# Passes shared with GpSimd and a planner that lets VectorE and GpSimd overlap, in a fused attention and two-layer kernel

## The chip, the cores and the metric

The kernel runs on one core of one Trainium2 chip. The metric is device time in microseconds (us) of one execution, and a variant is judged by the median of its runs. TensorE (PE in the profile, PEld for its weight loads) multiplies matrices, VectorE (DVE) and ScalarE (ACT) work element by element, GpSimd (POOL) does the same on tiles in SBUF, and SyncE (SP) issues all the DMAs.

## The reference

Attention over 4 batches and 8 heads, 576 positions of 64 values, with a causal window of 128 and a bias that falls linearly with distance; then a layer with a softmax gate and a normalisation over 1024 hidden values; then a gated layer with 2048 hidden values.

```python
def _attn_ref(q, k, v):
    scores = scale * np.matmul(q, k.transpose(0, 1, 3, 2))
    bias = slopes[:, None, None] * (-np.abs(rel).astype(np.float32))[None, :, :]
    mask = (rel >= 0) & (rel < window)
    scores = np.where(mask, scores + bias[None], -1000000000.0)
    attn = np.exp(scores - np.max(scores, axis=-1, keepdims=True))
    attn = attn / (np.sum(attn, axis=-1, keepdims=True) + 1e-09)
    return np.matmul(attn, v)

def _moe_ref(x, w_in, w_out, g_ln):          # 2304 tokens, 512 -> 1024 -> 512
    h = x @ w_in
    e = np.exp(h - np.max(h, axis=-1, keepdims=True))
    solu = h * (e / (np.sum(e, axis=-1, keepdims=True) + 1e-09))
    mu = np.mean(solu, axis=-1, keepdims=True)
    var = np.mean((solu - mu) ** 2, axis=-1, keepdims=True)
    return (((solu - mu) / np.sqrt(var + 1e-06)) * g_ln) @ w_out

def _moe2_ref(x, w_in, w_out):               # 2304 tokens, 512 -> 2048 -> 512
    h = x @ w_in
    return (h * (1.0 / (1.0 + np.exp(-h)))) @ w_out
```

## The kernel before

**Tiles.** The 2304 tokens are 18 blocks of 128 rows. A block goes through scores (`a_qk`), a pass that adds the bias and finds the row maximum (`a_max`), the exponential, a transposition of the weights (`a_parts`), the product with the values (`a_av`), a division (`a_evac`), the first matrix product (`m1_in`) and the normalisation (`layer_norm`). Two blocks form a chunk for `m1_out`, `m2_in` and `m2_out`.

**Splitting.** Each float32 operand of a large product is held as two half-precision tiles: the high part is a copy to half precision, the low part is what the copy left over. Three half-precision products then stand for one float32 product. So almost every tile passes through a "copy" (the helper `copy`, or `scaled` where a scale is applied) and a "low part" (the helper `combine`, a subtraction of two SBUF tiles, or a `scalar_tensor_tensor` of VectorE that scales and subtracts at once).

**Weights.** The weights come as 8-byte floats. `load_weight` loads 48 tiles into `stage` buffers, `decode` turns each into float32 (ScalarE L456, VectorE L458 and L460; one pair goes wholly through VectorE, L464 to L468), TensorE and VectorE compute a bound for the scale, and `split_weight` splits the tile: E_W says whether slot b takes the two-pass form of VectorE (`wh`, then L533) or the three-pass form (`wc` scales in place, `wh` copies, `wl` subtracts). Slots 0 to 7 are `w0`, 8 to 15 `w8`, 16 to 31 `w16`, 32 to 47 `w32`.

**Who does what, and in which order.** All work is entered into a list with its reads and writes. A planner in the program (`Sched.solve`) gives every piece to an engine and a place in that engine's order, by priorities (RANK, SLOPE, LATER by kind of work and block) and by a cost for each piece. PICK fixes the engine of most pieces: one letter per tile, V for VectorE, A for ScalarE, G for GpSimd. On the chip each engine works through its own order; semaphores make it wait for data. The planner before keeps one time, `port`, for pieces marked as holding a port that VectorE and GpSimd share: a marked piece of either engine begins only when the marked piece before it has ended:

```python
t = max(free[o.eng], o.ready, port if held else 0)
...
if held:
    port = t + o.cost
```

Marked are all of GpSimd's large passes, VectorE's copies and scalings, its subtractions in `combine`, and the `scalar_tensor_tensor` low parts. The decoding pass L460 is not marked, though it too reads two SBUF tiles.

**Lines that the steps below touch.** L342, L343: copies on ScalarE and VectorE. L347, L348, L350: scaled copies on ScalarE, VectorE, GpSimd. L354, L355: subtractions on VectorE and GpSimd. L533, L642: scale-and-subtract of weights and of values on VectorE. L688, L773: score and value products. L714: bias and maximum. L820, L920, L957, L984: the four large products.

Of the kernel before, what the change touches and what calls it, by code (L numbers as in the profile page):

```python
# [69 lines left out]

class Sched:
# [108 lines left out]
    def solve(self):  # L182
        free = {e: 580 for e in ("PE", "V", "A", "G", "SP")}
        dma_free = port = 0
# [31 lines left out]
        while n_left:  # L216
# [82 lines left out]
def fused_kernel(ctx, tc, qk, qn, kn, vt, rel, w_in, w_out, g_ln, w2_in, w2_out, out):  # L299
# [3 lines left out]
    s = Sched()  # L303
# [12 lines left out]
    def cv(n, fast=False):  # L316
        return 68 + (0.52 if fast else 1.045) * n
# [10 lines left out]
    def v(n, fn, r=(), w=(), fast=False, port=False):  # L328
        s.op([("V", cv(n, fast), fn, port or fast)], r, w)
# [30 lines left out]
    def transpose(fn, r=(), w=(), blocks=8):  # L360
        s.op([("SP", 1294, fn, False)], r, w, dma=165 * blocks)
# [81 lines left out]
    def decode(st, slot, j):  # L443
# [4 lines left out]
        def high():  # L448
            return st[:, :, 1]
# [4 lines left out]
        if DECODE[j // 2] == "A":  # L454

            act(512, lambda: A.activation(high().bitcast(F32), high().bitcast(F32), AF.Prelu,  # L456
# [3 lines left out]
            v(530, lambda: V.scalar_tensor_tensor(out=out(), in0=high(), scalar=3, in1=low(),  # L460
# [59 lines left out]
    def split_weight(name, slot0, n, cols, per_k=None):  # L520
        for j in range(n):
            def go(j=j):
# [8 lines left out]
                if E_W[b] == "V":  # L531
# [3 lines left out]
                      [(W, a), (W, b), src], [(W, b)], port=True)  # L535
# [100 lines left out]
    def v_split(i):  # L636
# [187 lines left out]
    def layer_norm(i):  # L824
# [120 lines left out]
    def m2_in(c, j):  # L945
# [18 lines left out]
        def flat(x):  # L964
# [83 lines left out]
    for c in range(NB // 2 + 1):  # L1048
# [7 lines left out]
        while n < until:  # L1056
# [12 lines left out]
RANK = {"aturn": 8190.5, "av": 1566.9, "evac": -3109.3, "exp": 5884.2, "gate": -1711.8, "in": -283.0, "in2": 763.1,  # L1069
        "load": -4397.6, "lparts": -1653.6, "max": 176.2, "max1": 339.6, "norm": -7961.4, "out": -1027.6,  # L1070
        "out2": 3298.4, "parts": -1379.1, "qk": 1402.7, "s0": -168.5, "s16": 369.8, "s32": 455.6, "s8": 3931.6,
        "share": -1605.8, "store": 2439.7, "table": -5196.2, "tav": 59.2, "tevac": -749.8, "texp": 4157.2,
        "tpar": 3201.3, "tscore": -1216.6, "tsub": 333.9, "vload": 753.3, "vnorm": -2520.6, "vsplit": 128.2,
        "w0": 1479.2, "w16": 76.9, "w32": 998.7, "w8": -63.2, "xturn": -869.5, "y": -1911.0}
SLOPE = {"aturn": 47.79, "av": -25.89, "evac": -5.68, "exp": 11.77, "gate": -21.88, "in": 36.34, "in2": -11.62,
         "load": 10.3, "lparts": 18.87, "max": -24.94, "max1": -2.34, "norm": -4.0, "out": 15.06, "out2": 30.48,
         "parts": -23.26, "qk": 32.18, "s0": 3.76, "s16": 1.95, "s32": 6.94, "s8": 26.54, "share": 17.85,
         "store": -34.37, "table": 17.51, "tav": -5.62, "tevac": 7.06, "texp": 19.15, "tpar": 25.04, "tscore": 5.66,
         "tsub": 13.31, "vload": 7.87, "vnorm": 15.99, "vsplit": 25.91, "w0": -6.05, "w16": 1.69, "w32": -8.51,
         "w8": -8.24, "xturn": 39.68, "y": -12.6}  # L1080
LATER = {("aturn", 1): 9.1, ("aturn", 2): -2.6, ("aturn", 3): 1.2, ("aturn", 6): -7.3, ("aturn", 7): -20.1,
         ("aturn", 9): -30.2, ("aturn", 11): -27.9, ("aturn", 12): -248.5, ("aturn", 13): 191.9, ("aturn", 14): 79.9,
         ("aturn", 15): -4.4, ("aturn", 16): 72.7, ("aturn", 17): -73.0, ("av", 0): -2.3, ("av", 1): -8.5,
         ("av", 2): 62.3, ("av", 5): 6.7, ("av", 6): 108.7, ("av", 8): -92.5, ("av", 12): 253.9, ("av", 13): -61.2,
         ("av", 16): -7.0, ("av", 17): 102.8, ("evac", 2): 2.1, ("evac", 3): 92.2, ("evac", 4): -25.0,
         ("evac", 5): -116.6, ("evac", 6): 0.4, ("evac", 7): -7.5, ("evac", 9): 269.9, ("evac", 12): 6.4,
         ("evac", 15): 61.8, ("evac", 16): 20.0, ("exp", 0): -2.6, ("exp", 1): -9.0, ("exp", 2): -239.6,
         ("exp", 4): 1.4, ("exp", 6): 95.0, ("exp", 8): 86.1, ("exp", 9): 34.4, ("exp", 10): 55.1, ("exp", 11): 11.9,
         ("exp", 12): -10.3, ("exp", 13): -121.4, ("exp", 14): 75.2, ("exp", 15): -38.3, ("exp", 16): 40.2,
         ("exp", 17): 91.8, ("gate", 2): -17.8, ("gate", 4): -56.2, ("gate", 10): -39.9, ("gate", 12): 66.8,  # L1090
# [138 lines left out]
```

## Time and profile before

| what | value |
|---|---|
| median of 3 runs | 731.22 us (730.71 to 733.2) |
| profiled execution, its own time | 729.44 us |
| its span in the profile | 727.5 us |
| TensorE's mean granted clock in it | 0.981 |
| instructions | 13956 |

The profile shows one execution. Its busy times are of each engine alone and overlap with each other; the table of stretches shows in which part of the run an engine is nearly always busy. A duration on VectorE or GpSimd includes time in which the instruction has begun and cannot go on, so the same instruction with the same shape is compared at its median and at its mean.

### The profile page before, as it was taken

The page shows a single profiled execution, that of the slowest core. Times are in us where ns is not written, and L with a number is a line of the kernel's source. Part 1 is how long each engine was busy: PE and PEld are TensorE (multiplying, and loading weights), DVE is VectorE, ACT ScalarE, POOL GpSimd, SP SyncE. Part 2 cuts the span into 40 slices and gives each one's busy share as a digit, 9 for nine tenths or more (in the row PEclk, how much of TensorE's full clock was granted, in tenths as well). Part 3 has the DMA queues.
Part 4 walks back from the last instruction along what each step waited for, and adds up shares of the span by engine and source line. Part 5 has one row for each costly group of instructions (what it writes and reads, how often), then busy time and mean ns, then how long its engine had stood idle before and what let it go on. Part 6 is the DMA issues. An engine that isn't in the chain of part 4 may idle for free.

```text
span 727.5 us, 13956 instructions
## 1 busy us (share of the span) xinstructions
PE 674.3 (93%) x5541; PEld 464.0 (64%) x5541; DVE 444.8 (61%) x1125; ACT 346.2 (48%) x738; POOL 138.5 (19%) x140
## 2 busy tenths in 40 slices
PE   4563688999999999999999999999999999999997
PEld 2432367778565577667766676678566777657853
DVE  3899999996897747553556657547672523321220
ACT  5687668575646635444454445525341422231231
POOL 1223034322443312130322112101010200100000
PEclk9996799999999999999999999999999999999999
DMA  9999985593535534251723454334250421100000
GB/s 309 346 247 273 241 199 134 131 231 89 99 78 103 130 73 81 53 114 31 145 59 73 82 107 90 91 56 73 44 102 1 68 65 30 30 30 1 1 30 29
DMA packets 142209, 75.82 MB, mean 104 GB/s; under 512 B 126656, under 2 KB 126784, under 8 KB 142144
## 3 DMA queue, kind: packets, MB, share of 16 engines
q1 hardware_dynamic: 142144, 74.94, 44.2%
q8 instruction: 43, 0.70, 0.4%
q14 instruction: 22, 0.18, 0.1%
HBM read 39.52 MB, written 4.72 MB: 61 GB/s over the span
## 4 chain that ended last, share of the span: by engine, by line
PE 79%; DVE 14%; ACT 3%; issue 2%; DMA 1%; POOL 0%; DVEq 0%; POOLq 0%; ACTq 0%
PE mm L984 25%; PE mm L957 23%; PE mm L920 12%; PE mm L820 11%; PE sa L688 4%; DVE W L460 3%; PE mm L773 2%; DVE stage L458 2%; DVE e L714 1%; PE gram L396 1%; DVE W L533 1%; PE sa L773 1%; DVE W L354 1%; DMA aT<-a 1%; DVE W L348 1%
## 5 line engine op out<-in xcount | busy, mean ns | idle before, releaser
L957 PE MATMUL mm<-y,W 128*128 128x256 f16 x1728 | 210.4, 273 | 1.1 <-DVE t L967 0.7
L984 PE MATMUL mm<-W,g 128*128 128x512 f16 x864 | 204.9, 379 | 0.0
L957 PEld LDWEIGHTS <-W 128*128 128x128 f16 x1728 | 167.0, 98 | 39.8 <-issue 2.0
L984 PEld LDWEIGHTS <-g 128*128 128x128 f16 x864 | 81.8, 98 | 78.7 <-issue 0.2
L820 PE MATMUL mm<-W,xT 128*128 128x512 f16 x432 | 105.2, 390 | 1.7 <-DVE xT L569 1.0
L920 PE MATMUL mm<-lnT,W 128*128 128x256 f16 x864 | 104.8, 273 | 0.0
L920 PEld LDWEIGHTS <-W 128*128 128x128 f16 x864 | 84.0, 98 | 19.7 <-issue 0.5
L719 ACT ACTIVATE e<-e,mx 128x256 f32<-128x256 f32 (+1 forms) x144 | 70.0, 487 | 45.9 <-DVE mx L714 43.3
L970 DVE SCALAR_TENSOR_TENSOR g<-t,g 128x512 f16<-128x512 f32 x72 | 55.5, 774 | 53.7 <-ACT g L969 53.3
L355 POOL TENSOR_TENSOR a<-e,a 128x512 f16<-128x512 f32 (+1 forms) x45 | 54.9, 1222 | 143.2 <-ACT a L342 65.8
L969 ACT ACTIVATE g<-t 128x512 f16<-128x512 f32 x72 | 45.0, 626 | 72.6 <-PE mm L984 61.1
L967 DVE SCALAR_TENSOR_TENSOR t<-t,mm 128x512 f32<-128x512 f32 x72 | 48.7, 682 | 48.3 <-ACT t L966 48.3
L966 ACT ACTIVATE t<-mm,cs 128x512 f32<-128x512 f32 x72 | 48.1, 680 | 62.5 <-PE mm L957 58.6
L820 PEld LDWEIGHTS <-xT 128*128 128x128 f16 x432 | 42.7, 100 | 47.6 <-issue 4.6
L688 PE MATMUL sa<-k,q 64*128 64x128 f32 x544 | 49.4, 312 | 17.1 <-DVE mx L714 12.2
L714 DVE CUSTOM_DVE_ANT_0 e<-sa,table 128x256 f32<-128x256 f32 (+1 forms) x144 | 53.9, 400 | 11.3 <-PE sa L688 6.3
L688 PEld LDWEIGHTS sa<-k,q 64*128 64x128 f32 x544 | 38.5, 202 | 29.1 <-DVE mx L714 15.7
L928 DVE SCALAR_TENSOR_TENSOR y<-mm,cs,y 128x512 f16<-128x512 f32 x18 | 13.3, 748 | 57.1 <-ACT y L925 57.1
L834 DVE TENSOR_REDUCE lnst<-mm 128x1 f32<-128x1024 f32 x18 | 22.0, 1220 | 42.0 <-PE mm L820 42.0
L848 POOL TENSOR_SCALAR lnst<-lnst 128x1 f32<-128x1 f32 x17 | 3.5, 203 | 214.0 <-ACT mm L845 214.0
L925 ACT ACTIVATE y<-mm,cs 128x512 f16<-128x512 f32 x18 | 12.2, 686 | 64.0 <-PE mm L920 56.3
L773 PEld LDWEIGHTS <-aT 128*128 128x128 f16 x816 | 32.9, 101 | 15.2 <-issue 8.6
(151 smaller groups left out, 707.9 us busy)
## 6 DMA issues: line engine op xcount, KB each, us to landing
stage<-in_moe_w_in_dram SPq DMA_DIRECT2D x24, 512.0 KB, 5.3
stage<-in_moe_w_out_dram SPq DMA_DIRECT2D x24, 512.0 KB, 4.5
k<-in_kn_dram SPq DMA_DIRECT2D x18, 256.0 KB, 2.9
q<-in_qn_dram SPq DMA_DIRECT2D x18, 256.0 KB, 3.1
vraw<-in_vt_dram SPq DMA_DIRECT2D x18, 256.0 KB, 3.8
out_dram<-t SPq DMA_DIRECT2D x18, 256.0 KB, 2.3
aT<-a SPq DMA_TRANSPOSE x72, 3.3
lnT<-ln SPq DMA_TRANSPOSE x34, 3.2
```

Of the source, the lines that this page charges most:

```text
L355: ("G", cg(n), lambda: G.tensor_tensor(dst(), a(), b(), op), True)], r, w, pick=pick)
L688: T.matmul(SA[:, j, off + sl * P:off + (sl + 1) * P], q[rows, p, :], k[rows, p, :], start=True, stop=sl not in blank)
L714: v(n + 20, lambda j=j: V.tensor_tensor_reduce(e[:, j, lo:lo + n], SA[:, j, off + lo:off + lo + n], table[:, 2 * p + j, o:o + n], -0.125, ...
L719: act(n, lambda j=j: A.activation(e[:, j, lo:lo + n], e[:, j, lo:lo + n], AF.Exp, bias=mx[:, j:j + 1], scale=-1.0, accum_out=rs[:, 2 * p + ...
L773: T.matmul(heads(i)[:, h // 4, h % 4, :], t[:, (2 * ha + j) * nh + c, :], vb[sl][:, h, hv, :], start=(n == 0), stop=(n == 3 * nh - 1))
L820: T.matmul(pt[:, half * 512:(half + 1) * 512], x[:, hx, k, :], W16(2 * k + half, hw), start=(k == 0 and hx + hw == 0), stop=(k == KD - 1 a ...
L920: T.matmul(pt[:, ct % 2], W16(8 + k, hw)[:, ct * P:(ct + 1) * P], l[:, hx * KF1 + k, :], start=(k == 0 and hw + hx == 0), stop=(k == KF1 - ...
L957: T.matmul(pt[:, mm], W16(16 + 4 * k + m // 4, hw)[:, (m % 4) * P:(m % 4 + 1) * P], y[:, hx, k, :], start=(k == 0 and hw + hx == 0), stop= ...
L966: act(512, lambda: A.activation(t.tile, flat(pt.tile), AF.Tanh, scale=cs[:, 0:1]), [pt, (cs, 0)], [t], extra=1)
L967: v(512, lambda: V.scalar_tensor_tensor(out=t.tile, in0=t.tile, scalar=1.0, in1=flat(pt.tile), op0=ALU.add, op1=ALU.mult), [t, pt], [t])
L970: v(512, lambda: V.scalar_tensor_tensor(out=flat(g[:, 1]), in0=t.tile, scalar=2.0 ** -16, in1=flat(g[:, 0]), op0=ALU.mult, op1=ALU.subtrac ...
L984: T.matmul(pt.tile, g[:, hg, mm, b * P:(b + 1) * P], W16(32 + m, hw), start=(m == 0 and hg + hw == 0), stop=(m == KF2 - 1 and hg == 1))
```

## The change

Copies of five kinds (`wh`, `ah`, `xh`, `lh`, `vg`) may go to GpSimd, as a `tensor_scalar` that multiplies by one twice. For blocks 0 to 5 (V_SPLIT is G) `v_split` has three passes instead of two: scale in place (`vc`), copy (`vg`), subtract (`vl`), each on the engine that PICK names. `m2_in` gets the same form for the gate, which GATE = "VVVVVVVVV" leaves unused. The planner drops `port`: VectorE and GpSimd begin when they are free, and a VectorE piece that begins while a GpSimd pass runs is charged a share of its own cost (1.0 for copies and scalings, 0.6 for subtractions, nothing for `scalar_tensor_tensor`), at most for as long as GpSimd's pass still lasts. Some costs in the planner change a little. PICK, E_W, ROOT, NORM, V_AT, RANK, SLOPE and LATER get new values, so the order of the work on every engine is a new one. No product of TensorE is added or removed, and the loads from HBM and transpositions are the same in number.

```diff
+SHARED_FAST, SHARED = 1.0, 0.6
@@ solve
-        dma_free = port = 0
+        dma_free = pool_until = 0
-                begins = max(free[other[0]], o.ready, port if other[3] else 0)
-                if begins + other[1] < max(t, port if alt[3] else 0) + alt[1]:
+                if max(free[other[0]], o.ready) + other[1] < t + alt[1]:
                     alt = other
-            o.eng, o.cost, o.fn, held = alt
-            t = max(free[o.eng], o.ready, port if held else 0)
+            o.eng, o.cost, o.fn, shares = alt
+            t = max(free[o.eng], o.ready)
+            if o.eng == "V":
+                o.cost += shares * min(o.cost, max(0.0, pool_until - t))
             o.done, o.start = True, t
             free[o.eng] = t + o.cost
-            if held:
-                port = t + o.cost
+            if o.eng == "G" and shares:
+                pool_until = t + o.cost
@@ copy
-              ("V", cv(n, True), lambda: V.tensor_copy(dst(), src()), True)], r, w, pick=pick)
+              ("V", cv(n, True), lambda: V.tensor_copy(dst(), src()), SHARED_FAST)] +
+             ([("G", cg1(n), lambda: G.tensor_scalar(dst(), src(), 1.0, 1.0, ALU.mult, ALU.mult), True)]
+              if pick[0] in ("wh", "ah", "xh", "lh", "vg") else []), r, w, pick=pick)
@@ v_split
+        if V_SPLIT[i] == "G":
+            scaled(("vc", i), 512, lambda: r.tile, lambda: r.tile, lambda: sv.tile, [r, sv], [r], True)
+            copy(("vg", i), 512, lambda: t[:, :, 0, :], lambda: r.tile, [r], [(t, 0)])
+            combine(("vl", i), 512, ALU.subtract, lambda: t[:, :, 1, :], lambda: r.tile, lambda: t[:, :, 0, :],
+                    [r, (t, 0)], [(t, 1)])
+            return
...
-E_W = "GGGGGGVGGVVGVVGGVGGVVGGVGVGGGGGVGVVGGGGVGVVGGGGG"
+E_W = "GVGGGGVGGVVGVVGGVGGGVGGVGVGGGGGVGVVGGGVVVVVGGGGG"
-ROOT = "GGGGGGGGGGGGGGVGGG"
-NORM = "VAAAGAAAGGAVVAVGGV"
+ROOT = "GGGGGGGVVGGGGGVGGG"
+NORM = "VAAAGAVAGGAGGVVVGV"
-PICK = {"wc": "AVGAAAAAAAAVAAGAAGAGAVAAAAAAAVGAVGAGGAVAGVAAAAGV",
-        "wh": "VAAAAAAAVAAAAVVVAAAVAVAVAAVAAVAAVVAAVAVAAVVVVAAA",
-        "wl": "VVVGVVGVGGGVGGGGGGGVGVGGGGGVGGVGGGGGVGVGVVGGGVVV", "vh": "AVAAAAVVAVAAVAVVVA",
-        "ah": "VAVAAVAVAAAAVVAVAAAVVAAAAAAVAVAVVVAAVVAVVVVVAAVVVVVVAVAVVAVAAVVAAVVVVVVV",
-        "al": "VGVGGGGGGGGVGGVGVGGVGGGVGGGGGGVGGVGGGVVGGGGVGVGVGGGGGVVVGVVGGVGVVGVVVGVV", "xh": "VAAAAVAVAAAAVVVVAA",
-        "xl": "GGGGGVVGVGGVVVVVVG", "lh": "VAVAVVVVVAAVVAVVVA", "ll": "V.VGVGGGGGGGGVGVGG"}
+PICK = {"vc": "VVAAAAAAAAAAAAAAAA", "vg": "AGAAAGAAAAAAAAAAAA", "vl": "GVGGGGGGGGGGGGGGGG",
+        "gl": "GGGGGGGGGGGGGGGGGGGGGGGGGGGGGGGGGGGGGGGGGGGGGGGGGGGGGGGGGGGGGGGGGGGGGGGG",
+        "wc": "VVAAGGAGAAAVAAAGAAAAAGAAVAGVVGAAAGAGVGVAVVAAVGGG",
+        "wh": "VVAGAAAAAAAVAAVVAAAVAAAAVAVGAVGAVAAGGGAVVVAGVAVA",
+        "wl": "VVGVGGGGGGGVGGVGGGGVGVGGGGGGVGVGVGGGVGVGVVGGGGGV", "vh": "AVAAAAAAAVAAVAVVAA",
+        "ah": "GGVVAGAAAGGAGVGGVGAVAVVGGGAAVGVAVVAAVVAVVVVVAAVVVVVVAVAAVAVAAVVAAVVVVGVV",
+        "al": "GVGGGGVGGGVVGGGGGVGGGGVGGVVVGVGGGVGGGVVGVGGVGVGVGGGGVVVVGVVGGVGVVVVVVGVV", "xh": "VAAAAGAAAAAAVVVVAA",
+        "xl": "GGGGVVGGVGGVGVVVVG", "lh": "VAVGAGGGVAAVVAVVVA", "ll": "V.GGVGGGGGGGGVGVGG"}
+V_SPLIT = "GGGGGGVVVVVVVVVVVV"
+GATE = "VVVVVVVVV"
-V_AT = [0, 1, 9, 10]
+V_AT = [0, 1, 5, 8]
```

## Rows read from the trace of the kernel before

**Rows 1.** The profile's page: busy us, share of the span, instructions.

```profile
PE 674.3 (93%) x5541; PEld 464.0 (64%) x5541; DVE 444.8 (61%) x1125; ACT 346.2 (48%) x738; POOL 138.5 (19%) x140
```

**Rows 2.** Busy time by stretch: from:to, length, busy us of each engine.

```profile
core 0: us, PE busy (x) PEld busy (x) DVE busy (x) ACT busy (x) POOL busy (x), PEclk, DMA share, GB/s
0.00:20.00 20.00, 7.87 (x53) 5.72 (x53) 8.30 (x38) 12.37 (x33) 2.42 (x15) 1.00 0.97 313
20.00:100.00 80.00, 48.96 (x394) 30.84 (x394) 75.55 (x200) 56.21 (x120) 19.75 (x19) 0.85 0.97 270
100.00:168.00 68.00, 62.48 (x602) 48.80 (x601) 66.79 (x158) 47.37 (x99) 23.40 (x21) 0.97 0.64 156
168.00:700.00 532.00, 531.28 (x4381) 366.90 (x4380) 289.41 (x723) 223.92 (x479) 92.97 (x85) 1.00 0.34 68
700.00:727.50 27.50, 23.70 (x122) 11.73 (x120) 4.74 (x7) 6.31 (x10) 0.00 (x0) 1.00 0.10 39
```

**Rows 3.** Groups of PE in 0 to 168 us: idle time before, releasers.

```profile
L688 PE MATMUL sa<-k,q 64*128 64x128 f32 x168 | 20.3, 364 | 17.1 <-DVE mx L714 12.2 <-DMA q<-in_qn_dram 5.0
...
L396 PE MATMUL gram<-W 128*128 128x128 bf16 x148 | 15.6, 252 | 10.9 <-DVE W L460 6.3 <-DVE sv L439 1.5 <-DVE accw2in L401 1.5
L773 PE MATMUL sa<-vs,aT 128*128 128x64 f16 x192 | 10.3, 214 | 7.0 <-DVE mx L714 6.7 <-DMA aT<-a 0.2
```

**Rows 4.** Timeline from 34 to 39 us: start, duration, instruction.

```profile
34.26 1.15 POOL L355 TENSOR_TENSOR a<-e,a 128x512 f16<-128x512 f32 x1
...
34.49 1.19 DVE L343 CAST a<-e 128x512 f16<-128x512 f32 x1
...
35.61 0.41 DVE L343 CAST x<-xm 128x512 f16<-128x512 f32 x1
```

**Rows 5.** Groups in 0 to 168 us by form: busy us, mean ns.

```profile
L460 DVE SCALAR_TENSOR_TENSOR W<-stage 128x512 uint32<-128x512 uint32 x46 | 35.9, 790 | 0.9 <-ACT stage L456 0.4
...
L458 DVE TENSOR_SCALAR stage<-stage 128x512 uint32<-128x512 uint32 x46 | 22.2, 488 | 0.0
...
L354 DVE TENSOR_TENSOR W<-W 128x512 f16<-128x512 f32 x10 | 8.2, 816 | 0.0
...
L533 DVE SCALAR_TENSOR_TENSOR W<-W,sw2in 128x512 f16<-128x512 f32 x6 | 5.8, 986 | 0.4 <-ACT W L347 0.4
...
L343 DVE CAST a<-e 128x512 f16<-128x512 f32 x7 | 3.7, 524 | 0.0
...
L466 DVE SCALAR_TENSOR_TENSOR W<-stage,W 128x512 uint32<-128x512 uint32 x2 | 3.1, 1528 | 0.0
```

**Rows 6.** Tile stage: durations ns min/median/max, first and last start.

```profile
L458 DVE TENSOR_SCALAR stage<-stage x46: 367/417/1380, 15.4 to 166.2; 128x512 uint32<-128x512 uint32 x46
L460 DVE SCALAR_TENSOR_TENSOR W<-stage x46: 670/680/2049, 16.0 to 167.1; 128x512 uint32<-128x512 uint32 x46
...
L468 DVE SCALAR_TENSOR_TENSOR W<-stage,W x2: 672/674/676, 159.4 to 166.5; 128x512 uint32<-128x512 uint32 x2
```

**Rows 7.** Single lines, 0 to 168 us: durations ns min/median/max.

```profile
L343 DVE CAST W<-W x7: 405/410/415, 39.7 to 136.9; 128x512 f16<-128x512 f32 x7
...
L354 DVE TENSOR_TENSOR W<-W x10: 673/676/1565, 40.4 to 136.3; 128x512 f16<-128x512 f32 x10
...
L533 DVE SCALAR_TENSOR_TENSOR W<-W,sw2in x6: 734/747/1640, 115.6 to 140.3; 128x512 f16<-128x512 f32 x6
...
L348 DVE TENSOR_SCALAR W<-W,gs x2: 471/474/476, 64.8 to 91.3; 128x512 f32<-128x512 f32 x1, 128x512 f16<-128x512 f32 x1
...
L350 POOL TENSOR_SCALAR W<-W,gs x1: 686/686/686, 59.9 to 59.9; 128x512 f32<-128x512 f32 x1
...
L355 POOL TENSOR_TENSOR W<-W x11: 1153/1161/2058, 46.6 to 137.4; 128x512 f16<-128x512 f32 x11
...
L642 DVE SCALAR_TENSOR_TENSOR vs<-vraw,sv,vs x5: 737/739/744, 17.6 to 119.3; 128x512 f16<-128x512 f32 x5
```

**Rows 8.** Groups of the whole run by line: a one-column VectorE pass of the root.

```profile
L859 DVE TENSOR_SCALAR lnst<-lnst 128x1 f32<-128x1 f32 x3 | 0.8, 271 | 0.1
```

**Rows 9.** Granted clock and busy time in one stretch of 20 us.

```profile
60.00:80.00 20.00, 8.92 (x48) 5.27 (x49) 18.80 (x46) 17.21 (x39) 6.21 (x7) 0.50 0.93 231
```

More of the change, by code (lines that the diff above doesn't have):

```diff
@@ L326, in cg1, with v @@
         return 215 + 1.05 * n
-    def v(n, fn, r=(), w=(), fast=False, port=False):
-        s.op([("V", cv(n, fast), fn, port or fast)], r, w)
+    def v(n, fn, r=(), w=(), fast=False):
+        s.op([("V", cv(n, fast), fn, SHARED_FAST if fast else 0.0)], r, w)
     def act(n, fn, r=(), w=(), extra=0):
@@ L360, in transpose @@
     def transpose(fn, r=(), w=(), blocks=8):
-        s.op([("SP", 1294, fn, False)], r, w, dma=165 * blocks)
+        s.op([("SP", 1340, fn, False)], r, w, dma=165 * blocks)
     W = Buf(const, [P, NSLOT + LAG, 512], F32, "W")
@@ L454, in decode @@
         if DECODE[j // 2] == "A":
[L456 removed]
+            act(580, lambda: A.activation(high().bitcast(F32), high().bitcast(F32), AF.Prelu,
                                           scale=2.0 ** 16, alpha=-2.0 ** 32), [(st, 0)], [(st, "high")])
@@ L534, in go @@
                                                           op0=ALU.mult, op1=ALU.subtract),
-                      [(W, a), (W, b), src], [(W, b)], port=True)
+                      [(W, a), (W, b), src], [(W, b)])
                     return
@@ L640, in v_split @@
         r = vraw[i]
+        if V_SPLIT[i] == "G":
[4 more added lines that the diff above has]
+            return
         scaled(("vh", i), 512, lambda: t[:, :, 0, :], lambda: r.tile, lambda: sv.tile, [r, sv], [(t, 0)])
         v(640, lambda: V.scalar_tensor_tensor(out=t[:, :, 1, :], in0=r.tile, scalar=sv.tile, in1=t[:, :, 0, :],
-                                              op0=ALU.mult, op1=ALU.subtract), [r, sv, (t, 0)], [(t, 1)], port=True)
+                                              op0=ALU.mult, op1=ALU.subtract), [r, sv, (t, 0)], [(t, 1)])
     kr, qr, es, aT, rsum = {}, {}, {}, {}, {}
@@ L968, in m2_in @@
                                               op1=ALU.mult), [t, pt], [t])
+        if GATE[c] == "G":
+            s.op([("G", cg1(512), lambda: G.tensor_scalar(t.tile, t.tile, 2.0 ** -16, 1.0, ALU.mult, ALU.mult), True)], [t], [t])
+            act(512, lambda: A.activation(flat(g[:, 0]), t.tile, AF.Copy), [t], [(g, 0)])
+            combine(("gl", 8 * c + j), 512, ALU.subtract, lambda: flat(g[:, 1]), lambda: t.tile, lambda: flat(g[:, 0]),
+                    [t, (g, 0)], [(g, 1)])
+            return
         act(512, lambda: A.activation(flat(g[:, 0]), t.tile, AF.Copy, scale=2.0 ** -16), [t], [(g, 0)])
         v(512, lambda: V.scalar_tensor_tensor(out=flat(g[:, 1]), in0=t.tile, scalar=2.0 ** -16, in1=flat(g[:, 0]),
-                                              op0=ALU.mult, op1=ALU.subtract), [t, (g, 0)], [(g, 1)], port=True)
+                                              op0=ALU.mult, op1=ALU.subtract), [t, (g, 0)], [(g, 1)])
     def m2_out(c, j):
@@ L1068 @@
 PITCH = 3.3
[L1069 to L1080, printed above, removed]
@@ new lines @@
+RANK = {"aturn": 8006.1, "av": 1879.0, "evac": -3847.7, "exp": 5373.2, "gate": -3029.2, "in": -1224.6, "in2": 374.3,
+        "load": -1508.8, "lparts": -2952.2, "max": 100.1, "max1": 508.5, "norm": -9709.7, "out": -1383.1,
+        "out2": 3304.4, "parts": -3030.2, "qk": 3092.8, "s0": -578.2, "s16": 532.0, "s32": 708.3, "s8": 2340.0,
+        "share": -2721.5, "store": 801.2, "table": -3894.2, "tav": -525.9, "tevac": -829.2, "texp": 3783.9,
+        "tpar": 3482.1, "tscore": -1673.9, "tsub": 148.6, "vload": 261.1, "vnorm": -2532.6, "vsplit": 1472.5,
+        "w0": 2055.6, "w16": 51.2, "w32": 1203.1, "w8": -344.2, "xturn": -1197.7, "y": -3339.4}
@@ new lines @@
+SLOPE = {"aturn": 49.72, "av": -29.68, "evac": -12.95, "exp": -0.09, "gate": -22.42, "in": 18.84, "in2": -12.17,
+         "load": 26.5, "lparts": 27.05, "max": -24.3, "max1": -24.39, "norm": 37.81, "out": 7.03, "out2": 36.78,
+         "parts": -17.17, "qk": 33.45, "s0": 10.09, "s16": -23.13, "s32": 3.75, "s8": -1.16, "share": -4.92,
+         "store": -14.75, "table": 15.94, "tav": 19.94, "tevac": 3.02, "texp": 13.72, "tpar": 17.57, "tscore": 15.48,
+         "tsub": 27.19, "vload": -0.9, "vnorm": 19.02, "vsplit": 18.14, "w0": -1.68, "w16": 16.51, "w32": -0.54,
+         "w8": -6.38, "xturn": 25.74, "y": -11.26}
```

90 lines of the change are left out of this document (46 added, 44 removed), and 40 rows, old and new, of the table LATER.

## The prediction

> **What bounds the kernel now.** I read the page of the profile first: TensorE is busy 93% of the span, VectorE 61%, GpSimd 19% [rows 1]. These shares hide two stages, so the busy times by stretch come next [rows 2]. From 168 us on TensorE is busy 531.28 of 532 us and VectorE 289.41: TensorE is the bound, and nothing that another engine saves there shows. Before 168 us it is the other way round: TensorE is busy 7.87 + 48.96 + 62.48 = 119.3 of 168 us, which leaves 48.7 us idle, while VectorE is busy 75.55 of 80 and 66.79 of 68 us. The first 20 us are different again: VectorE is busy for 8.30 us, and the DMA share is 0.97. So the run is a head of 168 us in which VectorE holds TensorE back (decoding and splitting the weights, beside the first five blocks), and a tail of some 560 us that is TensorE's. The change removes no product, so the time can fall only by what TensorE's 48.7 idle us in the head shrink (some 4 us at the very end apart), and rise by what they grow. Third, the idle time of TensorE in the head by what ended it [rows 3]: scores wait for the maximum pass of VectorE (12.2 us), value products too (6.7), the sums of squares for the decoding (6.3), together 25.2 us; 5.0 us wait for a load.
>
> Last the timeline, for how VectorE and GpSimd meet [rows 4]. A copy to half precision begins on VectorE at 34.49, while a subtraction of GpSimd runs from 34.26 to 35.41. It takes 1.19 us and ends at 35.68; the next copy of that shape takes 0.41. It is as if it had stood still until GpSimd was done. The durations by form show the same in sum [rows 5 to 7]: a mean above the undisturbed one, times the count, is time lost. L460: 46 x (790 - 680) = 5.1 us; L458: 46 x (488 - 417) = 3.3; L466, against the undisturbed L468: 2 x (1528 - 674) = 1.7; L533: 6 x (986 - 734) = 1.5; L354: 10 x (816 - 676) = 1.4; L343: 7 x (524 - 410) = 0.8. Together 13.8 us of VectorE's 150.6 busy us in the head, beside 2.42 + 19.75 + 23.40 = 45.6 us of GpSimd: 0.30 us of VectorE for each us of GpSimd.
>
> **The change, part by part, in the head.** Undisturbed prices on VectorE [rows 6, 7]: copy 0.41, scaled copy 0.47, subtraction 0.68, scale-and-subtract 0.74; on GpSimd one-input pass 0.69, subtraction 1.16. Half-size tiles count half, tiles of 1024 twice.
>
> Values, blocks 0 to 4 (block 5 comes behind the head): VectorE loses five scale-and-subtracts and one scaled copy (3.70 + 0.47) and gets two scaled copies and one subtraction (0.95 + 0.68): -2.5 us. GpSimd gets one copy and four subtractions: +5.3 us. The split has three passes instead of two: behind a ScalarE pass either way, 0.69 + 1.16 follow in place of 0.74, about a microsecond more before `a_av` may begin. I price this at nothing, since `a_av` also waits for the transposed weights; if that cover is gone it is 1 us for each of five blocks.
>
> Weights, by counting letters of E_W and PICK. `w0`: VectorE 5.7 to 4.2 us, -1.5; GpSimd two scalings, one copy, three subtractions more, +5.5. `w8`: VectorE +0.2, GpSimd -1.2. `w16`: VectorE -0.1, GpSimd three one-input passes, +2.1. `w32` is split behind the head (VectorE is idle nearly half of that time), where I price it at nothing; if it were early, it is some forty passes that trade engines with little net.
>
> Attention weights, blocks 0 to 4: of the copies four go from VectorE to GpSimd, five from ScalarE to GpSimd, two from ScalarE to VectorE, one back: VectorE -1.2, GpSimd +5.5 (nine, two of half size). Of the subtractions five go to GpSimd and four come back: VectorE -0.3, GpSimd +0.6. Normalised tiles: `ll` of block 2 to GpSimd: VectorE -1.4, GpSimd +2.3; `lh` of block 3 from ScalarE to GpSimd: +1.4.
>
> VectorE: -2.5 - 1.5 + 0.2 - 0.1 - 1.2 - 0.3 - 1.4 = **-6.8 us**. GpSimd: 5.3 + 5.5 - 1.2 + 2.1 + 5.5 + 0.6 + 2.3 + 1.4 = **+21.5 us**, from 45.6 to 67.1.
>
> What GpSimd's new passes take from VectorE: bounds are 0 (each runs beside passes of VectorE that are not held, such as the maximum pass) and 21.5 (each holds VectorE for its whole length). I take the measured 0.30, since the passes are of the same kind beside the same work: +6.5 us. So the shared work as such is worth -6.8 + 6.5 = -0.3 us. Many shares move, and little is won by them alone.
>
> Here the Trainium skill, page "SBUF — State Buffer", section "Who interferes with whom", speaks against the new planner: the port pair that the two engines share is an exclusive lock, held for a whole instruction, and the later one fully blocks; a VectorE instruction with two SBUF inputs is meant too. The trace agrees: the 0.41 us copy took 1.19 and ended 0.27 us after GpSimd's subtraction [rows 4]. The planner before charges just that; the new one charges at most a copy's own cost again, so 0.8 us in place of 1.19, and nothing to scale-and-subtracts and to L460, which lost 5.1 us [rows 5, 6]. By that rule alone the planner trusts overlap too much, and the sum is the first rival below.
>
> The order. Rearranged priorities remove no work, but TensorE's 25.2 us of waiting for VectorE [rows 3] depend on what VectorE does first. No row prices the new order; a gain is bounded by 25.2 us and a loss by about as much. The old planner never lets a marked pass begin on one engine beside the other's, so in its plan VectorE stands idle more than it need, even where the chip would finish the pass earlier or GpSimd would be the one to wait. I take a fifth of the 25.2 as gain, -5 us: a choice between -25 and +25, leaning to gain because GpSimd stands idle in 122 of the head's 168 us and now takes the late passes (`vl`, `w0`) off an engine whose queue is full.
>
> Small parts, with one answer: two more roots on VectorE are 2 x 9 one-column passes of at most 0.27 us [rows 8], 4.9 us, and NORM's five moves lie in the tail where VectorE is busy 54% of the time, so nothing; without that cover they would cost their length. V_AT lets ScalarE's squares for batches 2 and 3 come earlier: same work, and the loads still wait for their buffers in the same order. GATE adds nothing. The changed costs act only through the order.
>
> Sum: 729.4 (profiled) - 0.3 - 5 = 724.1; the median of the runs lies 1.8 above the profiled execution, so **726 us**, 5 below the 731.2 shown.
>
> **The rivals.**
>
> *GpSimd holds VectorE more often (slower).* The new planner no longer keeps the two apart, so the rate rises from 0.30. It decides at (13.8 + 6.8 + 5) / 67.1 = 0.38: above that the kernel is slower. At 0.5 the held time is 33.6, 19.8 more than now: 19.8 - 6.8 - 5 = +8, **739 us**. For it: L460, L458 and most splitting passes can be held, and the order avoids this no longer. Against it: only part of VectorE's passes can be held, and those that may be go partly to GpSimd.
>
> *No change.* What VectorE sheds comes back as held time (-0.3 above), the order finds nothing, because the first 20 us wait for loads and from 100 to 168 us TensorE is already busy 92% [rows 2]: **731 us**, 729 to 733.
>
> *A larger gain.* The new order sets GpSimd's passes beside maximum passes and reductions from PSUM, and the rate falls to 0.2: held time 13.4, -0.4; -0.4 - 6.8 - 5 = -12: **719 us**. A fuller TensorE could also keep its higher clock: from 60 to 80 us it was granted 0.50 (1.2 in place of 2.4 GHz) with 8.92 us busy [rows 9], so up to 4.5 us less work there, behind a stretch in which it often stood idle.
>
> **How the numbers follow.** Forecast (722 to 729) 0.33, larger gain 0.17, no change 0.18, slower 0.32. Within 0.3% (2.2 us) is about what a measurement of this kernel can't tell from no change; so faster 0.50, same 0.18, slower 0.32. The slower case reaches from 733 to 746; for 8 in 10 I leave out a tenth above 741 and somewhat less below 716. The likeliest case's own range is 722 to 729.
>
> **What the changed profile would show.** The first step is right if VectorE's undisturbed work in the head is some 7 us less, and GpSimd's busy time there about 65 us. The held time (mean against median of L460, L458, L354, L533) tells the rate: near 0.3 as forecast, under 0.25 the larger gain, above 0.38 slower. The order shows in when TensorE becomes continuously busy (now about 160 us), in its idle time before that (48.7), and in the waits of L688 and L773 for L714. I am wrong if TensorE has new gaps in the tail, from GpSimd subtractions of 1.16 us that come late for a transposition, or if blocks wait for `vl`.

## The result, and the profile after

The changed kernel takes **737.20 us** (median of 4 runs, 736.89 to 738.55); the kernel before took 730.99 beside it (4 runs). The ratio is **1.0082 [1.0059 to 1.0105]**: some 6 us slower. The profiled execution took 737.25 us, its span is 735.5, 8.0 more than before.

The page of the changed kernel first (busy us, share of the span, instructions), against [rows 1]:

```profile
PE 675.9 (92%) x5541; PEld 465.2 (63%) x5541; DVE 438.3 (60%) x1121; ACT 338.0 (46%) x724; POOL 172.3 (23%) x174
```

GpSimd took 33.8 us more, VectorE lost 6.5, ScalarE 8.2. TensorE did the same products. Where it stands idle is read from the stretches, against [rows 2] (from:to, length, busy us of each engine; the last line but one is an extra stretch inside the one above it):

```profile
0.00:20.00 20.00, 7.59 (x49) 5.30 (x49) 8.28 (x36) 12.76 (x33) 5.64 (x19) 1.00 0.94 302
20.00:100.00 80.00, 48.14 (x387) 30.53 (x387) 73.74 (x193) 51.24 (x113) 29.27 (x29) 0.85 0.94 259
100.00:168.00 68.00, 61.17 (x576) 45.46 (x576) 66.80 (x153) 45.24 (x93) 37.87 (x35) 0.95 0.70 173
168.00:700.00 532.00, 527.40 (x4349) 365.91 (x4347) 283.83 (x734) 220.91 (x475) 99.50 (x92) 1.00 0.33 68
168.00:240.00 72.00, 69.11 (x589) 47.49 (x587) 55.92 (x138) 40.48 (x89) 33.86 (x33) 1.00 0.43 95
700.00:735.50 35.50, 31.61 (x187) 18.02 (x185) 5.64 (x9) 7.80 (x12) 0.00 (x0) 0.99 0.08 30
```

In the head TensorE does 7.59 + 48.14 + 61.17 = 116.9 us of work where it did 119.3 (1010 matmuls in place of 1042): 2.4 us are pushed behind 168 us. Behind 168 us it then idles 4.6 of 532 us, where it idled 0.7: 3.9 us of new gaps, 2.9 of them before 240 us. The same stretch of the kernel before had next to none:

```profile
168.00:240.00 72.00, 71.84 (x618) 47.12 (x617) 58.27 (x140) 43.00 (x97) 26.92 (x24) 1.00 0.48 96
```

Add the 1.6 us by which TensorE's busy time differs (675.9 - 674.3), and 2.4 + 3.9 + 1.6 = 7.9 is the growth of the span. So the loss lies in two places: a little less done in the head, and gaps just behind it.

GpSimd is busy 5.64 + 29.27 + 37.87 = 72.8 us in the head (before 45.6). What that does to VectorE stands in the forms in 0 to 168 us (count, busy us, mean ns) ...

```profile
L466 DVE SCALAR_TENSOR_TENSOR W<-stage 128x512 uint32<-128x512 uint32 x44 | 35.4, 809 | 0.5
L464 DVE TENSOR_SCALAR stage<-stage 128x512 uint32<-128x512 uint32 x44 | 26.2, 600 | 0.0
...
L360 DVE TENSOR_TENSOR W<-W 128x512 f16<-128x512 f32 x8 | 7.4, 920 | 0.0
```

... against the medians of the whole run (ns min/median/max, first and last start):

```profile
L464 DVE TENSOR_SCALAR stage<-stage x46: 374/421/2345, 15.0 to 174.6; 128x512 uint32<-128x512 uint32 x46
L466 DVE SCALAR_TENSOR_TENSOR W<-stage x46: 670/686/1649, 15.8 to 175.1; 128x512 uint32<-128x512 uint32 x46
```

L464 (before L458) loses 44 x (600 - 421) = 7.9 us where it lost 3.3 [rows 5, 6], L466 (L460) 44 x (809 - 686) = 5.4 where it lost 5.1, L360 (L354) 8 x (920 - 678) = 1.9 where it lost 1.4. One decoding pass took 2345 ns in place of 421. Mean against median, times the count, added over all of VectorE's groups in the head, makes 22.7 us held, where the same sum of before makes 15.9. The sum depends on which passes are grouped for the median: other groupings give 20 to 25 us after and 12 to 18 before, and 5 to 11 more after. The last decoding pass starts at 175.1 us, before at 167.1 [rows 6].

The waits of TensorE in the head grew with it, against [rows 3]:

```profile
L700 PE MATMUL sa<-k,q 64*128 64x128 f32 x168 | 21.4, 380 | 20.1 <-DVE mx L726 14.6 <-DMA q<-in_qn_dram 5.5
...
L402 PE MATMUL gram<-W 128*128 128x128 bf16 x136 | 14.9, 250 | 11.7 <-DVE W L466 8.6 <-DVE accwout L521 1.8 <-DVE sv L445 1.3
L785 PE MATMUL sa<-vs,aT 128*128 128x64 f16 x228 | 12.1, 211 | 0.9 <-DVE mx L726 0.9
```

Scores wait 14.6 us for the maximum pass (before 12.2), the sums of squares 8.6 us for the decoding (6.3); only the value products wait less (0.9 in place of 6.7). Together 24.1 us in place of 25.2.

A gap behind 168 us, in the timeline of the changed kernel (start, duration, instruction, [idle before]):

```profile
223.56 2.57 POOL L361 TENSOR_TENSOR ln<-e,ln 128x1024 f16<-128x1024 f32 x1
...
224.76 1.66 DVE L347 CAST a<-e 128x512 f16<-128x512 f32 x1
...
226.34 0.68 DVE L979 SCALAR_TENSOR_TENSOR t<-t,mm 128x512 f32<-128x512 f32 x1
...
227.07 0.18 PE L393 MATMUL mm<-shrr,ones 128*128 128x2 bf16 x1 [1.01 <-DVE t L979]
```

A subtraction of GpSimd ends at 226.13. VectorE's copy beside it takes 1.66 us in place of 0.41, so L979, which empties a PSUM tile, ends at 227.02 and TensorE has waited 1.01 us. L979 itself is not slowed; it stands in the queue behind a pass that is. The waits of TensorE from 168 to 240 us name it (total, times, longest):

```profile
PE mm L969 <- DVE t L979: 1.3, 2, 0.8
PE mm L393 <- DVE t L979: 1.0, 1, 1.0
```

### The profile page after: what moved, and what is told of

It reads as the page before. It is cut to its first block, busy times and chain, and to the rows that moved or that the text cites. A ratio compares the mean times of both kernels' runs of the same rounds, so it can differ in the third digit from the quotient of the medians.

```text
span 735.5 us, 13984 instructions
## 1 busy us (share of the span) xinstructions
PE 675.9 (92%) x5541; PEld 465.2 (63%) x5541; DVE 438.3 (60%) x1121; ACT 338.0 (46%) x724; POOL 172.3 (23%) x174
## 4 chain that ended last, share of the span: by engine, by line
PE 75%; DVE 15%; issue 2%; DMA 2%; ACT 1%; POOL 1%; SPq 0%; DVEq 0%; ACTq 0%; POOLq 0%
PE mm L1002 24%; PE mm L969 23%; PE mm L932 11%; PE mm L832 10%; PE sa L700 3%; DVE W L466 3%; DVE stage L464 2%; PE mm L785 2%; DVE e L726 2%; DMA aT<-a 1%; DVE W L539 1%; DVE W L360 1%; DVE g L988 1%; DVE t L979 1%; DMA xT<-x 1%
## 5 line engine op out<-in xcount | busy, mean ns | idle before, releaser
L969 PE MATMUL mm<-y,W 128*128 128x256 f16 x1728 | 207.5, 273 | 3.6 <-DVE W L360 1.8
L832 PE MATMUL mm<-W,xT 128*128 128x512 f16 x432 | 101.9, 389 | 0.9 <-DMA xT<-x 0.9
L932 PE MATMUL mm<-lnT,W 128*128 128x256 f16 x864 | 102.2, 273 | 0.3 <-POOL W L361 0.2
L979 DVE SCALAR_TENSOR_TENSOR t<-t,mm 128x512 f32<-128x512 f32 x72 | 48.8, 683 | 67.3 <-ACT t L978 67.0
L361 POOL TENSOR_TENSOR a<-e,a 128x512 f16<-128x512 f32 (+1 forms) x40 | 47.2, 1182 | 155.6 <-DVE a L347 99.6
L848 ACT ACTIVATE e<-mm,lnst,sig 128x1024 f32<-128x1024 f32 x18 | 21.6, 1199 | 51.0 <-DVE lnst L847 50.9
L361 POOL TENSOR_TENSOR ln<-e,ln 128x1024 f16<-128x1024 f32 x13 | 29.9, 2299 | 42.0 <-DVE ln L347 33.7
```

Of the source, the lines that this page charges most:

```text
L361: ("G", cg(n), lambda: G.tensor_tensor(dst(), a(), b(), op), True)], r, w, pick=pick)
L832: T.matmul(pt[:, half * 512:(half + 1) * 512], x[:, hx, k, :], W16(2 * k + half, hw), start=(k == 0 and hx + hw == 0), stop=(k == KD - 1 a ...
L932: T.matmul(pt[:, ct % 2], W16(8 + k, hw)[:, ct * P:(ct + 1) * P], l[:, hx * KF1 + k, :], start=(k == 0 and hw + hx == 0), stop=(k == KF1 - ...
L969: T.matmul(pt[:, mm], W16(16 + 4 * k + m // 4, hw)[:, (m % 4) * P:(m % 4 + 1) * P], y[:, hx, k, :], start=(k == 0 and hw + hx == 0), stop= ...
L979: v(512, lambda: V.scalar_tensor_tensor(out=t.tile, in0=t.tile, scalar=1.0, in1=flat(pt.tile), op0=ALU.add, op1=ALU.mult), [t, pt], [t])
```

## The experiments

Four questions: how much of the time is GpSimd holding VectorE, how much is GpSimd being late, how much is the new order, and can a part of the change be undone. In all runs but the last two the order of both kernels is kept and pieces are changed only where they are emitted. "Before" is the kernel before, run beside it on the same chip; e1 to e4 ran on one chip, e5 to e7 on a second, e8 and e9 on a third, so across these groups only ratios are compared.

| run | median us | before us | ratio |
|---|---|---|---|
| e1: after, GpSimd's passes short | 722.32 | 731.85 | 0.9868 [0.9854 to 0.9883] |
| e2: before, GpSimd's passes short | 724.23 | 731.85 | 0.9905 [0.9884 to 0.9926] |
| e5: after, short, GpSimd as long busy | 725.44 | 732.15 | 0.9914 [0.9887 to 0.9942] |
| e6: before, short, GpSimd as long busy | 723.73 | 732.15 | 0.9893 [0.9869 to 0.9917] |
| e3: after, GpSimd's copies to ScalarE | 739.14 | 731.85 | 1.0103 [1.0088 to 1.0118] |
| e4: before, with after's copies on GpSimd | 735.11 | 731.85 | 1.0044 [1.0027 to 1.0061] |
| e7: after, five `vl` to VectorE | 740.18 | 732.15 | 1.0110 [1.0087 to 1.0133] |
| e8: after, planned with the whole wait | 728.33 | 732.27 | 0.9949 [0.9933 to 0.9966] |
| e9: before, searched anew | 730.57 | 732.27 | 0.9976 [0.9962 to 0.9990] |

**e1 and e2: GpSimd's passes cut to an eighth, in both kernels.** Copies and subtractions fill the rest of their result with zeros, scalings leave it as it was.

```diff
-              ("G", cg(n), lambda: G.tensor_tensor(dst(), a(), b(), op), True)], r, w, pick=pick)
+              ("G", cg(n), lambda: short_sub(dst(), a(), b(), op), True)], r, w, pick=pick)
+    def short_sub(dst, a, b, op):
+        G.tensor_tensor(ends(dst)[0], ends(a)[0], ends(b)[0], op)
+        G.memset(ends(dst)[1].bitcast(F32), 0.0)
```

> The changed kernel with its own order kept piece for piece, but every large GpSimd pass works on an eighth of its columns and the rest of its output is filled with zeros (the values are not the reference's): GpSimd can hold VectorE only briefly. Theory H (the loss is VectorE held by GpSimd in places where the plan counted too little): the 22.7 us of held time in the head go, and the new order is then as good as planned or better, 715 to 723 us, below the same cut of the kernel before. Theory O (the new order is worse whatever GpSimd does, through longer chains and late pieces): it gains no more than the kernel before does by the same cut and stays some 6 us above it.

> The kernel before with the same cut of its GpSimd passes and its own order kept (an eighth of the columns, the rest zeros; the values are not the reference's). Both theories: its 13.8 to 16 us of held time in the head go, 721 to 728 us. The two theories differ in how this stands to the cut version of the changed kernel: H puts it above, O puts it about 6 us below.

With GpSimd's passes short both kernels gain, and the changed one gains more: it is now the faster by 0.9905 - 0.9868 = 0.37%, 2.7 us of 731. That is what the new order and the lighter VectorE are worth here. GpSimd is not out of the way, though: with its zeros it is still busy 44.5 us in the head (72.8 uncut) and 28.7 (45.6 uncut), so part of its lateness is left in, and more of it in the changed kernel. Held time in the head, by mean against median as above, is 3.2 and 0.8 us. The stretch from 0 to 168 us of e1 ...

```profile
0.00:168.00 168.00, 127.81 (x1132) 92.13 (x1133) 137.50 (x398) 115.74 (x246) 44.47 (x138) 0.92 0.90 237
```

... and of e2:

```profile
0.00:168.00 168.00, 126.57 (x1108) 92.12 (x1109) 135.92 (x400) 117.14 (x252) 28.67 (x84) 0.91 0.83 229
```

TensorE does 127.8 and 126.6 us of work in the head, in place of 116.9 and 119.3. This cut takes two things away at once, the holding and part of the time for which GpSimd's results are late. The next pair parts them in part.

**e5 and e6: the same cut, with filler.** Behind each cut pass GpSimd runs one-column passes of about the time saved (the root of one column, some 0.55 us alone), which hold nobody.

```diff
+    def idle(long, short):
+        for _ in range(long):
+            G.tensor_tensor(fill[:, 1:2], fill[:, 0:1], half.tile, ALU.pow)
+        for _ in range(short):
+            G.tensor_scalar(fill[:, 1:2], fill[:, 0:1], 1.0, 1.0, ALU.mult, ALU.add)
```

> The changed kernel, order kept, GpSimd's large passes again on an eighth of their columns with zeros in the rest, but each followed by one-column GpSimd passes (548 and 190 ns, beside which VectorE's two-tile passes kept their length in both traces) so that GpSimd is occupied for about as long as in the uncut kernel (values not the reference's). Theory H1 (VectorE being held is the loss): stays near the cut version, 722 to 727 us. Theory H2 (GpSimd's own length is the loss: low parts that come late): goes back toward the changed kernel, 733 to 738 us.

> The kernel before with the same treatment and its own order. H1: near its cut version, 724 to 727 us, and no better than the changed kernel treated alike. H2: back to 729 to 732 us.

GpSimd's busy time in the head is as in the uncut kernels. In e5 ...

```profile
0.00:168.00 168.00, 123.52 (x1104) 88.31 (x1105) 137.50 (x396) 114.43 (x245) 73.08 (x205) 0.93 0.89 237
```

... it is 73.1 us (72.8 uncut), and in e6 ...

```profile
0.00:168.00 168.00, 124.82 (x1101) 90.84 (x1103) 135.86 (x397) 116.56 (x251) 49.20 (x123) 0.83 0.85 229
```

... 49.2 (45.6 uncut). The held time is nearly gone all the same (about 4 and 1 us by the same sum). In e5 the two decoding passes show it at once, 469 and 688 ns in the mean (600 and 809 uncut):

```profile
L493 DVE TENSOR_SCALAR stage<-stage 128x512 uint32<-128x512 uint32 x46 | 21.4, 469 | 0.4 <-DMA stage<-in_moe_w_out_dram 0.4
...
L495 DVE SCALAR_TENSOR_TENSOR W<-stage 128x512 uint32<-128x512 uint32 x46 | 31.5, 688 | 1.0 <-ACT stage L491 0.4
```

The filler makes GpSimd's next piece late, but not the result of the piece before it. In e5 VectorE begins on a tile at 134.95, when the zeros behind GpSimd's copy have ended (134.91), while the filler runs on:

```profile
134.45 0.24 POOL L379 TENSOR_SCALAR W<-W 128x64 f16<-128x64 f32 x1
134.63 0.28 POOL L380 MEMSET W<- 128x224 f32 x1
...
134.88 0.19 POOL L371 TENSOR_SCALAR fill<-fill 128x1 f32<-128x1 f32 x1
...
134.95 0.69 DVE L388 TENSOR_TENSOR W<-W 128x512 f16<-128x512 f32 x1 [1.38 <-POOL W L380]
```

So the result of a subtraction of 512 columns is there after about 0.6 us (0.31 and 0.28 for pass and zeros), where it took 1.16.

The four runs and the two kernels make a sum, in per cent of 731 us. *Holding* (uncut against filled): after 1.0082 - 0.9914 = 1.68%, 12.3 us; before 1 - 0.9893 = 1.07%, 7.8 us. So 4.5 us more; in it stands, beside VectorE's held time, that each uncut result comes later and that GpSimd's own passes are held. *Length* (filled against short; only GpSimd's queue being longer): after 0.9914 - 0.9868 = 0.46%, 3.4 us; before 0.9893 - 0.9905 = -0.12%, nothing that can be told from zero. So 4.3 us more. *Order and relief* (short against short): -2.7 us. 4.5 + 4.3 - 2.7 = +6.1 us, the measured loss. By the intervals the first two are uncertain by about 3 us each and the third by 2. That GpSimd's long passes turn a gain of 2.7 us into a loss of 6.1 is shown; how much of it is VectorE held and how much GpSimd's results late is not, since the two names do not part them cleanly. With GpSimd as busy as uncut but nearly nothing held, the changed kernel is not the faster one either: 0.9914 against 0.9893, whose intervals overlap. The range expected for e6 (724 to 727) was missed narrowly, and so was "no better than the changed kernel treated alike". The gaps behind 168 us go with the cut: in e5 TensorE is busy 71.82 of the 72 us to 240, in the changed kernel 69.11.

**e3: the 28 copies that GpSimd does go to ScalarE**, the rest of the change stays.

```diff
-                o.fn()
+                to = moved(o)
+                fn = o.fn if to is None else next((x[2] for x in o.every if x[0] == to), o.fn)
+                fn()
+def moved(o):
+    return "A" if o.tag and o.eng == "G" and o.tag[0] in ("wh", "ah", "xh", "lh", "vg") else None
```

> The changed kernel, order kept piece for piece, but the 28 copies that it gives to GpSimd run on ScalarE at the same places in the order. H: GpSimd's busy time in the head falls by some 12 us and VectorE's held time by about 0.3 of it, 4 us, so 732 to 735 us. O: the copies are not the cause, 736 to 739 us, more if ScalarE becomes late.

A miss for the theory that held time alone sets the end, at the upper end of the other range: GpSimd is busy 9.8 us less in the head (62.95), held time falls from 22.7 to 18.9, and the kernel is no faster (1.0103 against 1.0082, whose intervals overlap). VectorE's waits from 20 to 168 us, in e3 ...

```profile
DVE e L735 <- POOL a L370: 1.6, 2, 1.1
...
DVE W L356 <- POOL W L370: 1.0, 1, 1.0
DVE t L988 <- ACT t L987: 0.9, 1, 0.9
```

... and in the changed kernel:

```profile
DVE e L726 <- POOL a L361: 1.8, 2, 1.3
```

In e3 the last two are new, and VectorE's waits for GpSimd and for ScalarE in the head rise from 1.8 and 1.1 to 4.4 and 2.5 us: what VectorE no longer stands still inside an instruction, it waits ahead of one, for data of GpSimd and of ScalarE. The order of VectorE's queue is fixed, so a microsecond freed ahead of a late operand is not saved.

**e4: the kernel before, with its copies on GpSimd where the changed one has them**; its order and every other letter stay.

```diff
+              ("V", cv(n, True), lambda: V.tensor_copy(dst(), src()), True),
+              ("G", cg1(n), lambda: G.tensor_scalar(dst(), src(), 1.0, 1.0, ALU.mult, ALU.mult), True)], r, w, pick=pick)
+    return "G" if o.tag and o.tag[0] in on_pool and on_pool[o.tag[0]][o.tag[1]] == "G" else None
```

> The kernel before, order kept piece for piece, but the copies that the changed kernel gives to GpSimd run there, at the places of the order before (the value splitting stays as it was). H: each copy adds 0.7 us of GpSimd that holds VectorE for 0.3 of it and saves 0.41 only where it came from VectorE, and pieces behind it come later: 732 to 737 us. O: the sharing as such is harmless, 729 to 732 us.

Slower by 0.44%, 3.2 us, with 54.2 us of GpSimd in the head and 17.4 held. Sharing the copies costs time in the old order too.

**e7: five value subtractions (`vl` of blocks 0, 2, 3, 4 and 5) go back to VectorE.**

```diff
+    return "V" if o.tag and o.eng == "G" and o.tag[0] == "vl" else None
```

> The changed kernel, order kept, but the subtractions of the value splitting (vl of blocks 0, 2, 3, 4, 5) run on VectorE at the same places. H1: GpSimd's time in the head falls by about 6 us and the held time by about 2, while VectorE gets 5 x 0.68 us: 735 to 738 us, no clear gain. If the splitting in three passes with a late low part is what delays the blocks, 731 to 734 us.

No gain again, and more than the 735 to 738 us expected (1.0110 against the changed kernel's 1.0082; the intervals overlap): GpSimd 67.3 us in the head, held 20.3, but VectorE has five passes of 0.68 us more, and TensorE does 113.55 us in the head. In e3 and here, moving letters in a kept order did not mend the plan; other letters were not tried.

**e8 and e9: the plan made anew.** e8 keeps the new freedoms (copies on GpSimd, splits in three passes) and charges in the planner nearly what the traces show: a pass that begins beside a shared pass of the other engine waits until that is over (less 0.2 us; in the traces of the two kernels VectorE's held passes went on 0.13 to 0.21 us ahead of GpSimd's end), either way round, the decoding and the scale-and-subtracts included. RANK, SLOPE, LATER and PICK were then searched anew. e9 is the control: the kernel before with its own rules, and the same tables searched anew, each order scored with the whole wait charged. So e9 has half of e8's new charge too, in the search and not in the planner.

```diff
+            def first(a):
+                t = max(free[a[0]], o.ready)
+                return max(t, lock[a[0]]) if a[3] and a[0] in lock else t
-            if o.eng == "V":
-                o.cost += shares * min(o.cost, max(0.0, pool_until - t))
+            if held and o.eng in "VG":
+                o.cost += max(0.0, lock[o.eng] - t)
+                other = "G" if o.eng == "V" else "V"
+                lock[other] = max(lock[other], t + o.cost - 200)
```

> The changed kernel with the same permissions (copies on GpSimd, values of blocks 0 to 5 in three passes, its E_W, NORM, ROOT), but the planner charges the whole wait in both directions, for scale-and-subtracts and the decoding pass too (until 0.2 us before the other's end, as in the traces), and RANK, SLOPE, LATER and PICK were searched anew by the planner's own total under that charge. Theory H1 (the failed step is the planner's charge): faster than both kernels, 717 to 724 us. Theory S (sharing these passes with GpSimd can't pay on this chip): 731 us or more.

> The kernel before with its own planner and permissions (no copies on GpSimd, values in two passes), RANK, SLOPE, LATER and PICK searched anew, each order scored with the whole wait charged. If a well-charged order is worth more than the sharing: 720 to 726 us, within some 3 us of the kernel with sharing. If the sharing is what helps: near 731 us.

e8 is faster than both kernels: 0.9949, and against the changed kernel 0.9949 / 1.0082 = 0.987, some 10 us by the two ratios. At 728.33 us it falls between the two ranges that were expected, short of the 717 to 724 of H1. Its stretches:

```profile
0.00:168.00 168.00, 122.58 (x1079) 86.11 (x1080) 147.01 (x387) 116.17 (x250) 64.38 (x72) 0.87 0.87 225
168.00:240.00 72.00, 70.18 (x567) 46.74 (x565) 62.43 (x152) 40.88 (x94) 30.10 (x29) 0.98 0.46 109
```

and its two decoding passes in the head:

```profile
L469 DVE TENSOR_SCALAR stage<-stage 128x512 uint32<-128x512 uint32 x44 | 21.0, 485 | 0.3 <-DMA stage<-in_moe_w_out_dram 0.3
...
L471 DVE SCALAR_TENSOR_TENSOR W<-stage 128x512 uint32<-128x512 uint32 x44 | 33.2, 760 | 1.0 <-ACT stage L467 0.5
```

GpSimd still does 64.4 us in the head, 18.8 more than before, yet L469 is held for 44 x (485 - 420) = 2.9 us in place of 7.9, and TensorE gets 122.6 us of work done there. The last decoding pass starts at 182.3 us, later than in either kernel: late decoding as such is not the loss. Gaps just behind the head remain (70.18 of 72 us busy). How much of e8's gain is its charge and how much the search can't be parted well: the old sharing, searched with the whole wait in the score (e9), gives 0.9976 [0.9962 to 0.9990], about half, and its interval touches e8's. It lies near the 731 us expected if the sharing is what helps, not in the 720 to 726 of a well-charged order alone; but the 2.2 us between e9 and e8 are hardly clear of noise. The changed planner, searched anew under its own charge, was not run, so that its charge is what spoils the plan is argued, not shown.

## Why the prediction was wrong

The forecast was 726 us, the result 737.2: the first rival ("GpSimd holds VectorE more often", 739) came true in sign and size, but not by the road that it named: it reached 739 by a rate of 0.5 and a loss only above 0.38, and the rate stayed near 0.3. That its size fits is luck.

**The first step: right.** VectorE's undisturbed work in the head was forecast to fall by 6.8 us. By the sums above it fell from 150.6 - 15.9 = 134.7 to 148.8 - 22.7 = 126.1, 8.6 us, of which two pairs of decoding passes (2.2 us) only slipped behind 168 us.

**Held time: right.** Forecast +6.5 us in the head at 0.30 for each us of GpSimd; measured 22.7 - 15.9 = +6.8 (the groupings above: 5 to 11), at 22.7 / 72.8 = 0.31 (0.28 to 0.34). The rate did not rise to the 0.38 at which the rival was to decide. GpSimd's busy time was 72.8 in place of 67.1; its own passes are held too and grow, which explains some 2.4 us of this (mean against median of its groups: 6.4 us in the head, before 4.0), and the rest was not traced. In run time the extra holding cost at most about 4.5 us (e5, e6), later results included. For each us held in the head, at most about 7.8 / 15.9 = 0.5 reached the end before and 12.3 / 22.7 = 0.5 after. The Trainium skill, page "SBUF — State Buffer", section "Who interferes with whom", calls the shared port an exclusive lock on which the later engine fully blocks, passes with two SBUF inputs included. The traces agree (1.66 in place of 0.41 us beside GpSimd's subtraction; 7.8 and 12.3 us gone once GpSimd's large passes are), and e8, which charges that to the plan, is the fastest of the kernels that do the whole work.

**The order and VectorE's relief: the step that failed.** The prediction took "a fifth of the 25.2 as gain, -5 us" for the order and added VectorE's -6.8 us in full as run time, -11.8 together. With GpSimd's passes short they are worth -2.7 (e1 against e2), and with GpSimd as long busy nothing that shows (e5 against e6). Two errors lie in it; no run parts them. A microsecond off VectorE was counted as one off the run, where a held one counted at most half; and the -5 had no row. The waits on which it was to act stayed: 25.2 us became 24.1, the value products' gone, the scores' and the decoding's grown. The argument that the old planner left VectorE idle is one about its plan: on the chip VectorE was busy 142.3 of the 148 us from 20 to 168 [rows 2]. The new plan set GpSimd's passes beside the decoding, L464 above all (7.9 us held in place of 3.3).

**GpSimd's later results: the second step that failed.** "I price this at nothing, since `a_av` also waits for the transposed weights", and `w32` and what lies behind the head at nothing too. A longer GpSimd queue cost 3.4 us in the changed kernel and nothing that shows in the one before (e5 against e1, e6 against e2), +4.3 between them. Which of its results is the late one is not shown: moving the copies (e3) or `vl` (e7) alone did not bring it back, and in the changed kernel's trace no matmul of `a_av` waits for GpSimd's `vs`, so the prediction's sign "if blocks wait for `vl`" did not come.

In sum, forecast against measured: relief and order -11.8 against -2.7, held +6.5 against +4.5, lateness 0 against +4.3, where the last two are parted only roughly. The errors are +9.1 - 2.0 + 4.3 = +11.4, the distance from 726 to 737. The largest, +9.1, is the one that the runs show best.

**The tail: the sign of being wrong came.** The prediction called 168 us onward TensorE's, where "nothing that another engine saves there shows", and named new gaps there as what would make it wrong. They came, 3.9 us, though mostly by another way than it said: L979, behind a held copy, more than a late transposition. Busy 54% of the tail, VectorE still has moments in which a PSUM tile waits on it.

**The clock: not supported.** The "larger gain" counted up to 4.5 us from a fuller clock. From 60 to 80 us the granted clock did rise, from 0.50 [rows 9] to 0.74, and a matmul of the scores took 351 ns in place of 457; TensorE was busy there 13.0 us in place of 8.9; the head as a whole did less all the same (116.9 us of work in place of 119.3). More on this below.

## What to carry to other kernels

Where VectorE and GpSimd share passes with operands in SBUF, charge the whole wait, both ways, to the plan: the one plan here that did (e8) was the fastest, though the search has a part in that. Price a relief of the bounding engine by what of its time reaches the end (here at most about half), price what comes later by the longer queue of the engine that takes the work, and a new order at nothing unless a row says which wait it removes. A share of 54% over a long stretch is no cover for a 1 us pass that comes between two PSUM evictions.

## What the runs showed of the hardware that was not expected

**Not every GpSimd pass holds VectorE.** The one-column root of GpSimd (128x1, about 0.55 us) does not: e5 has GpSimd as busy as the uncut kernel and about 4 us held in place of 22.7, and where only one-column passes ran beside them the two decoding passes took 414 to 425 and 676 to 689 ns, their undisturbed lengths. The hold is mutual, too: GpSimd's subtraction of 512 columns takes 1.15 us alone and up to 2.2 us where it begins beside a shared pass of VectorE; the one of 1024 columns in the timeline above took 2.57, where the median of its 13 is 2.18. VectorE's passes with a PSUM operand, like L979 at 226.34 (0.68 us), keep their length: all 72 of L979 took 632 to 691 ns.

**Early in the run the clock row and the matmuls disagree.** From 20 to 50 us the row of e3 says 0.50 (1.2 in place of 2.4 GHz) ...

```profile
20.00:50.00 30.00, 15.70 (x122) 10.22 (x121) 25.56 (x61) 19.37 (x39) 13.77 (x13) 0.50 0.94 277
...
L709 PE MATMUL sa<-k,q 64*128 64x128 f32 x24 | 3.7, 457 | 2.0 <-DVE mx L735 2.0
```

... and that of the changed kernel 1.00:

```profile
20.00:50.00 30.00, 15.66 (x123) 10.42 (x124) 25.46 (x59) 16.67 (x34) 14.70 (x13) 1.00 0.91 279
...
L700 PE MATMUL sa<-k,q 64*128 64x128 f32 x24 | 3.7, 457 | 2.2 <-DVE mx L726 2.2
```

A matmul of the scores takes 457 ns in both. That is what it took at 0.50 in the kernel before from 60 to 80 us (457); from 168 to 700 us, at 1.00, it takes 289 in the changed kernel. So the 1.00 of this early row is not borne out, and the two rows can't be used to say what a half clock costs. Nor do mean clocks of whole runs, which contain this stretch: of the 28 executions of the kernel before beside e1 to e9, the ten with a mean clock below 0.96 have a median of 732.5 us and the eighteen above it 731.6.
